# Batch 2's k and v as six tokens to a partition, with no fifth-slot load, and k's permutation in four pieces

## The chip, the cores and the metric

The kernel runs on one core of a Trainium2 chip. The metric is the device time of one execution in microseconds (us). Before the change the median of seven runs is 293.79 us, the lowest 292.74 us and the highest 295.01 us.

## What is computed

The inputs q, k, v have 8 batches, 8 heads, 576 tokens and 64 features to a head, in f32. The first stage is an attention without a softmax, the second a feed-forward block with a residual.

```python
kv  = einsum('bhsd,bhse->bhde', k, v)                # 64 x 64 for each batch and head
out = einsum('bhsd,bhde->bhse', q, kv)
out = out / sqrt(mean(out*out, -1) + 1e-6) * g_norm  # norm over the 64 features of a head
x   = out with the heads side by side                # 8 x 576 rows of 512
xn  = (x - mean) / sqrt(var + 1e-6) * g_ln           # layer norm over 512
y   = x + relu(xn @ w_ch1) @ w_ch2                   # 512 -> 2048 -> 512
```

## The kernel before

**Tiles.** The 4608 rows are 36 tiles of 128. A batch has 576 tokens: four full tiles (token slots 0 to 3 of a partition) and a half tile, the "fifth slot", of 64 tokens. Two neighbouring batches share one tile for their two half tiles, so tile 8 is the fifth slot of batches 0 and 1, and tiles 9 to 12 are batch 2's. The order of the tiles is batch 0's four (0 to 3), batch 1's four (4 to 7), tile 8, batch 2's four, batch 3's four, their shared tile, and so on. Tiles 0 to 7 go through the feed-forward one at a time ("fine" groups, L629), later ones in blocks of four (L644). The second product (`m2`, L663) is always by tile, in four groups of four matmuls.

**One batch.** GpSimd (POOL) loads q, k and v and casts them to bf16 on the way. k has to lie token slot first in `kp`. For batches 0 and 1 the load puts six consecutive tokens on each of 96 partitions (`kb`, `vb`), with all 576 tokens in one load, and a copy (`k_permute`, L404) brings k into `kp`. For batch 2 four tokens go on each of 128 partitions, 512 tokens in all, and the last 64 tokens come by a second small load, `load_fifth` (L262): k's straight into slot 4 of `kp`, v's into `v5`. The other 64 partitions of that slot of `kp` are zeroed by a memset on POOL (L760). From batch 3 on, `load_slots` (L275) writes k into `kp` slot by slot and no copy is needed. q of batch 2 comes into `qb` and is permuted by two copies on ScalarE (ACT) (`q_permute`, L410), and its half tile is loaded by a `load_fifth` too. `kv_mm` (L456) multiplies k by v: 6 matmuls with 96 rows to a pair of heads for batches 0 and 1 (24 in all), 5 with 128 rows for the others (20).

q is needed transposed, as `qT`. Batch 0's slots are turned on TensorE (PE). Batch 1's slots 2 and 3 are turned by one DMA transpose issued by SyncE (SP), and its slot 4 by another; `late_turns` holds that last one back, in the plan, behind a main group of the feed-forward (L999). Batch 2 is turned by one DMA transpose for all slots, after its permutes and q's fifth slot. `t_out` (L478) then multiplies `qT` by the batch's kv; tile 8 needs slot 4 of both batch 0 and batch 1, eight matmuls.

**What sets the order.** Nothing is ordered at run time: each engine has a fixed list, written out by `run_plan` (L108) before the kernel runs. A step has an engine, a planned occupation, a key (lower is more urgent) and the steps it depends on. At each turn the plan takes, on each engine, the step that can start first; among those that can start at the same moment the lowest key wins, and among equal keys the one that was added first. Loads and DMA transposes book a common planned server one after another, at rates written by hand (L193 and L314):

```python
rate6, rate4, rate1 = 400.0, 395.0, 305.0
begin = max(server, t + s.occ + lat)
server = begin + wk
s.done = begin + wk + tail
```

`lag` adds a number of microseconds to a load's planned arrival before ACT or PE may be planned to use it. A POOL load waits for the eighth load before it. The keys that matter below: the out matmuls of tile 8 and `kv_mm` of batch 2 both have key 40, which is also the key of the first `m2` group of tile 4, and ties go in the order in which the steps are added (that group, then tile 8's out, L838, then batch 2's `kv_mm`, L803). In the list each engine waits for the data of an instruction, with all that stands behind it.

Of the kernel before, what the change touches and what calls it, by code (L numbers as in the profile page):

```python
# [14 lines left out]
def kernel(  # L15
# [11 lines left out]
    nc = tc.nc  # L27
# [22 lines left out]
    NEAR = 0.35  # L50
    BANKS = {"mm": 4, "out": 2, "kvt": 2}
    WARM_FROM = 1.3
    HALVED = (0,)
    SCALED = (0, 1)
    SPLIT_STORE = (23, 25)
# [42 lines left out]
    def add(eng, occ, dur, key, deps, fn, dma=None, alloc=None, main=False, lag=0.0):  # L98
        s = Step()
        s.eng, s.occ, s.dur, s.key, s.fn = eng, occ, dur, key, fn  # L100
        s.deps = [d for d in deps if d is not None]
        s.dma, s.alloc, s.main, s.frees, s.behind = dma, alloc, main, None, None
        s.start = s.done = None
        s.lag = lag
        steps.append(s)
        return s
# [131 lines left out]
    kv_pack = [consts.tile([128, HP, 128], bf16, name=f"kv_pack{i}") for i in range(3)]  # L238

    def kv_view(buf, b):  # L240
        if b < 2:
            return buf[b % 2][0:96, :].rearrange("p (h t d) -> p h t d", h=H, t=6)
        return buf[b % 2][:, 0:H * 4 * D].rearrange("p (h t d) -> p h t d", h=H, t=4)

    def load_kv(buf, src, b, h0=0, h1=H):
        t = 6 if b < 2 else 4
        n = 576 if b < 2 else 512
        def fn():
            nc.gpsimd.dma_start(  # L249
                kv_view(buf, b)[:, h0:h1, :, :].rearrange("p h t d -> p h (t d)"),  # L250
                src[b, h0:h1, 0:n, :].rearrange("h (p t) d -> p h (t d)", t=t))
        return fn, n * (h1 - h0) * 256
# [9 lines left out]
    def load_fifth(dst, src, b):  # L262
        def fn():
            nc.gpsimd.dma_start(
                dst[fifth(b), :, :], src[b, :, 512:576, :].rearrange("h p d -> p h d"))
        return fn, 64 * H * 256
# [49 lines left out]
    load = {}  # L316
# [25 lines left out]
    def pool_load(name, fnb, rate=425.0, deps=()):  # L342
        fn, nb = fnb
        s = add_dma("POOL", 0, deps, fn, nb, rate)
        load.setdefault(name, []).append(s)
# [58 lines left out]
    def k_permute(eng, b, h0, h1):  # L404
        src = kv_view(kb, b)
        t = src.shape[2]
        copy(eng, kp[b % 2][0:src.shape[0], 0:t, h0:h1, :],
             src[:, h0:h1, :, :].rearrange("p h t d -> p t h d"))
# [46 lines left out]

    def kv_mm(b, hps):  # L456
        ps = psum.tile([128, HP, 128], f32, tag="kvt", name="kv_ps", bufs=BANKS["kvt"])
        p, last = (slice(0, 96), 5) if b < 2 else (slice(0, 128), 4)
        for hp in hps:
            for t in range(last + 1):  # L460
                nc.tensor.matmul(  # L461
                    ps[:, hp, :],
                    lhsT=kp[b % 2][p, t, 2 * hp:2 * hp + 2, :].rearrange("p h d -> p (h d)"),
                    rhs=(v5[b % 2][:, 2 * hp:2 * hp + 2, :] if b >= 2 and t == 4
                         else kv_view(vb, b)[:, 2 * hp:2 * hp + 2, t, :]),
                    start=(t == 0), stop=(t == last))
            att[b]["kv", hp] = ps
# [253 lines left out]
    def plan_batch(b):  # L721
        p = pos[FIRST[b]]
        ok = okey[FIRST[b]]
        kperm = []
        if b == 1:
            for h0, h1 in ((0, 4), (4, 8)):
                kperm.append(add("ACT", 1.2, 1.35, p - 18, load["k", 1],
                                 lambda h0=h0, h1=h1: k_permute(nc.scalar, 1, h0, h1)))
            for t in range(5):
                key = (p - 17 + 3 * t) if t < 4 else pos[8] - 40  # L730
                if t < 4:
                    qperm = add("ACT", *act_cost(512), key, load["q", 1],
                                lambda t=t: q_permute(nc.scalar, 1, t, t + 1))
                    qread = qperm
                else:
                    qperm = load["q", 1, 4][0]
                if t < 2:
                    add_q_turn_pe(1, t, [qperm, z1[1]], key + 1, ("DVE", "ACT")[t % 2])
                elif t > 2:
                    add_q_turn_dma(1, *((2, 4) if t == 3 else (4, 5)), [qperm, z1[1]],  # L740
                                   key + 1 if t == 3 else pos[8] - 29)
            vdeps = load["v", 1]
            adone[1]["qread"] = qread
            adone[1]["qfree"] = adone[1]["qT", 4][0]
        else:
            f = FIRST[b]
            def gate(n):

                if b >= 3:
                    m, i = divmod(n, 4)  # L750
                    pool_do(0.1, lambda: nc.gpsimd.tensor_copy(  # L751
                        mark, blk[m]["xT"][:, 0, i * 128:i * 128 + 1]), done[n]["xT"])
            def gate_turn():
                if b >= 3:
                    pool_do(0.1, lambda: nc.gpsimd.tensor_copy(
                        mark, att[b - 1]["qT"][:, 0, 0:1]), [adone[b - 1]["qfree"]])
            dk = [adone[b - 2]["kvmm"]]
            if b < 4:

                pool_do(0.5, lambda: nc.gpsimd.memset(kp[b % 2][no_fifth(b), 4, :, :], 0.0), dk)  # L760
            gate(f - 8 if b > 3 else 5)
            gate_turn()
            by_slot = b >= 3
            if by_slot:
                pool_load(("k", b), load_slots(kp[b % 2], k, b), rate1, dk)
            else:
                pool_load(("k", b), load_kv(kb, k, b), rate4, dk)
            pool_load(("k", b), load_fifth(kp[b % 2][:, 4, :, :], k, b), 180.0, dk)
            def some_q():
                gate(f - 7 if b > 3 else 6)  # L770
                if by_slot:
                    pool_load(("q", b), load_slots(qp[b % 2], q, b), rate1, [adone[b - 2]["qfree"]])
                else:
                    pool_load(("q", b), load_q(b, 0, 4), rate4, [adone[b - 1]["qread"]])
                pool_load(("q", b), load_fifth(qp[b % 2][:, 4, :, :], q, b), 180.0,
                          [adone[b - 2]["qfree"]])
            def some_v():
                gate(f - 6 if b > 3 else 7)
                pool_load(("v", b), load_kv(vb, v, b), rate4, dk)
                pool_load(("v", b), load_fifth(v5[b % 2], v, b), 100.0, dk)  # L780
            for load_some in (some_v, some_q) if b == 2 else (some_q, some_v):
                load_some()
            for h0, h1 in ((0, 4), (4, 8))[by_slot * 2:]:
                kperm.append(add("ACT", 0.85, 1.0, ok - 16, load["k", b][0:1] + dk,
                                 lambda h0=h0, h1=h1: k_permute(nc.scalar, b, h0, h1)))
            qperm = []
            for t0, t1 in ((0, 2), (2, 4))[by_slot * 2:]:
                qperm.append(add("ACT", 0.85, 1.0, ok - 14, load["q", b][0:1] + [
                    adone[b - 2]["qfree"]], lambda t0=t0, t1=t1: q_permute(nc.scalar, b, t0, t1)))
            for x in kperm + qperm:  # L790
                x.lag = 4.0 if b == 2 else 6.0
            kperm += load["k", b]
            turn = add_dma("SP", ok - 12, qperm + load["q", b] + (
                adone[b - 3].get("outs", []) if b >= 3 else []),
                           lambda: q_turn_dma(b), 2.6e3, 1.0, occ=2.98, lat=0.25, tail=0.42)
            for t in range(5):
                adone[b]["qT", t] = [turn]
            adone[b]["qfree"] = turn
            turn.lag = 5.0 if by_slot else 0.0
            adone[b]["qread"] = qperm[-1] if qperm else None  # L800
            vdeps = load["v", b]
        outs_before = adone[b - 3].get("outs", []) if b >= 3 else []
        s = add("PE", 1.12 if b > 1 else 1.34, 1.35 if b > 1 else 1.57, (p - 17.5 if b == 1 else ok - 4), vdeps + kperm,  # L803
                lambda: kv_mm(b, range(HP)), alloc="kvt")
        a = add("DVE", 0.34, 0.38, (p - 17 if b == 1 else ok - 2), [s, z1[4], z1[5]] + outs_before,
                lambda: kv_out(b, 0, HP, nc.vector, False))
        a2 = add("DVE", 0.34, 0.38, (p - 17 if b == 1 else ok - 2), [a], lambda: kv_out(b, 0, HP, nc.vector, True))
        s.frees = a2
        s.lag = 5.0 if b > 2 else 2.0 if b == 2 else 0.0
        adone[b]["kvmm"] = s  # L810
        adone[b]["kv"] = [a2]
# [243 lines left out]
```

## Time and profile before

| | |
|---|---|
| median of seven runs | 293.79 us |
| the profiled execution | 293.79 us, its span 292.0 us |
| granted TensorE clock | 1.00 |
| PE busy | 284.2 us of the span |
| VectorE (DVE), ScalarE (ACT), GpSimd (POOL) busy | 164.8, 142.5, 65.9 us |
| q and kb loads of 512 KB from issue to landing | 18.6 us and 17.9 us |
| 64 KB loads into `kp` (k's fifth slots), to landing | 7.9 us |

The profile's page has the busy time of each engine, the span in 40 slices, and the chain of work that ended last, followed back from the end. The trace gives each engine's instructions in order of time: start, length, engine, line, operation, tile written and read, count, and in brackets an idle time before it and what ended that. PE's lengths are modelled and overlap: back to back, a 128-column matmul starts some 0.056 us after the one before and a 512-column one some 0.216 us after. "PEld" is the load of the stationary operand, and SPq is SP's queue of DMA issues.

### The profile page before, as it was taken

What the parts mean: (1) busy time and instruction counts of PE and PEld (TensorE: products, weight loads), DVE (VectorE), ACT (ScalarE), POOL (GpSimd) and SP (SyncE); (2) the same over time, 40 slices, a digit from 0 to 9 for tenths busy, and PEclk for the clock granted to TensorE, in tenths of its full rate; (3) what the DMA queues carried; (4) which work ended last, traced back from release to release, by engine and by line L of the source; (5) the groups of instructions that cost most, each with busy time, mean ns of one, the idle gap of its engine ahead of it and who ended that gap; (6) DMA issues with size and microseconds to landing.
All of it is one profiled execution on the core that took longest, in us unless ns stands there. A gap on an engine that the chain in (4) does not pass through costs nothing.

```text
span 292.0 us, 5193 instructions
## 1 busy us (share of the span) xinstructions
PE 284.2 (97%) x2046; PEld 162.7 (56%) x2074; DVE 164.8 (56%) x362; ACT 142.5 (49%) x288; POOL 65.9 (23%) x93
## 2 busy tenths in 40 slices
PE   8999989999999999999999999999999999999995
PEld 6879844977745445444544445444544444444444
DVE  2596029487983997557655775477557755320022
ACT  2279955797756612761276127612761177017400
POOL 8974230107309004502260406000000000000000
PEclk9999999999999999999999999999999999999999
DMA  6999999958999978998999399912101310120012
GB/s 92 178 196 206 204 199 177 250 69 108 180 212 103 171 109 199 116 169 175 131 135 167 88 188 115 191 55 92 54 18 56 90 54 18 56 88 20 2 72 73
DMA packets 108716, 35.60 MB, mean 122 GB/s; under 512 B 87187, under 2 KB 104467, under 8 KB 108692
## 3 DMA queue, kind: packets, MB, share of 16 engines
q0 software_dynamic: 72624, 18.35, 66.0%
q1 hardware_dynamic: 35828, 16.79, 26.0%
q8 instruction: 16, 0.26, 0.4%
q10 hardware_dynamic: 240, 0.13, 0.2%
q14 instruction: 8, 0.07, 0.1%
HBM read 36.70 MB, written 9.44 MB: 158 GB/s over the span
## 4 chain that ended last, share of the span: by engine, by line
PE 85%; DMA 7%; POOL 6%; issue 1%; ACT 0%; DVE 0%; POOLq 0%
PE mm_ps L663 41%; PE mm_ps L644 33%; DMA qb<-in_q_dram 7%; PE mm_ps L629 5%; PE out_ps L484 3%; PE kv_ps L461 2%; POOL qp L270 1%; POOL w L354 1%; POOL vb L249 1%; POOL kb L249 1%; PE xT_ps L579 1%; POOL w L356 0%; PE qT_ps L420 0%; ACT qp L400 0%; POOL identity masks.py:197 0%
## 5 line engine op out<-in xcount | busy, mean ns | idle before, releaser
L663 PE MATMUL mm_ps<-w,m 128*128 128x512 bf16 (+2 forms) x592 | 128.1, 368 | 0.7
L644 PE MATMUL mm_ps<-xT,w 128*128 128x512 bf16 x436 | 100.0, 379 | 0.6
L651 ACT ACTIVATE m<-mm_ps 128x512 bf16<-128x512 f32 x112 | 66.8, 597 | 50.8 <-PE mm_ps L644 48.5
L663 PEld LDWEIGHTS <-m 128*128 128x128 bf16 x608 | 57.2, 98 | 60.6
L644 PEld LDWEIGHTS <-w 128*128 128x128 bf16 x448 | 43.1, 98 | 48.8
L519 DVE TENSOR_REDUCE ss<-sq 128x8 f32<-128x512 f32 (+1 forms) x37 | 24.8, 669 | 48.2 <-ACT sq L510 48.0
L670 DVE SCALAR_TENSOR_TENSOR x<-mm_ps,rstd,x 128x512 f32<-128x512 f32 (+2 forms) x38 | 27.2, 719 | 40.6 <-PE mm_ps L663 40.6
L510 ACT ACTIVATE sq<-out_ps 128x512 f32<-128x512 f32 (+1 forms) x37 | 21.6, 584 | 45.9 <-PE out_ps L484 45.9
L629 PE MATMUL mm_ps<-xT,w 128*128 128x128 bf16 x512 | 30.6, 219 | 0.0
L629 PEld LDWEIGHTS <-w 128*128 128x128 bf16 x512 | 29.2, 98 | 0.8
L572 DVE SCALAR_TENSOR_TENSOR xc<-x,mv,gl 128x512 bf16<-128x512 f32 (+1 forms) x38 | 27.3, 723 | 1.2
L514 DVE TENSOR_TENSOR xg<-out_ps,gn 128x512 f32<-128x512 f32 x34 | 23.2, 683 | 0.2
L636 ACT ACTIVATE m<-mm_ps 128x512 bf16<-128x512 f32 x32 | 18.4, 596 | 3.1 <-PE mm_ps L629 2.9
L751 POOL COPY mark<-xT 128x1 bf16<-128x1 bf16 x15 | 6.5, 431 | 57.0 <-DMA xT<-xc 51.5
L523 ACT ACTIVATE rms<-ss,eps_attn 128x8 f32<-128x8 f32 (+1 forms) x37 | 11.1, 300 | 14.4 <-DVE ss L519 14.3
L550 DVE TENSOR_TENSOR x<-xg,inv 128x512 f32<-128x512 f32 x24 | 16.6, 691 | 0.8
L566 DVE BATCH_NORM_STATS2 stats<-x 128x6 f32<-128x512 f32 x24 | 16.5, 690 | 0.5
L484 PEld LDWEIGHTS <-qT 128*128 128x128 bf16 x160 | 11.4, 98 | 6.5 <-ACT qT L400 0.5
L484 PE MATMUL out_ps<-kv_pack,qT 128*128 128x128 bf16 x160 | 14.5, 219 | 0.3
L472 DVE CAST kv_pack<-kv_ps 64x256 bf16<-64x256 f32 x14 | 5.9, 422 | 11.9 <-PE kv_ps L461 11.8
L461 PEld LDWEIGHTS <-kp 128*128 128x128 bf16 (+1 forms) x168 | 10.7, 102 | 2.4 <-issue 0.4
L461 PE MATMUL kv_ps<-vb,kp 128*128 128x128 bf16 (+1 forms) x144 | 11.3, 227 | 0.4 <-DMA vb<-in_v_dram 0.4
(69 smaller groups left out, 183.1 us busy)
## 6 DMA issues: line engine op xcount, KB each, us to landing
out_dram<-x SPq DMA_DIRECT2D x30, 256.0 KB, 2.6
w<-in_moe_w_ch_dram POOLq DMA_DIRECT2D x8, 512.0 KB, 12.2
vb<-in_v_dram POOLq DMA_DIRECT2D x6, 512.0 KB, 10.8
kp<-in_k_dram POOLq DMA_DIRECT2D x5, 512.0 KB, 8.5
qp<-in_q_dram POOLq DMA_DIRECT2D x5, 512.0 KB, 10.1
out_dram<-x SPq DMA_DIRECT2D x10, 128.0 KB, 2.3
qb<-in_q_dram POOLq DMA_DIRECT2D x2, 512.0 KB, 18.6
qp<-in_q_dram POOLq DMA_DIRECT2D x10, 64.0 KB, 9.0
```

Source lines behind the costliest of these rows:

```text
L461: nc.tensor.matmul(ps[:, hp, :], lhsT=kp[b % 2][p, t, 2 * hp:2 * hp + 2, :].rearrange("p h d -> p (h d)"), rhs=(v5[b % 2][:, 2 * hp:2 * hp ...
L484: nc.tensor.matmul(o3[:, hp, :], lhsT=att[b]["qT"][:, 4 * t + hp, :], rhs=kv_pack[b % 3][:, hp, :], start=(i == 0), stop=(i == len(bs) - 1))
L510: nc.scalar.activation(sq[:, h0:h1, :], st[n]["ps", h0][:, h0:h1, :], func=AF.Square)
L514: nc.vector.tensor_mul(xg[:, h0:h1, :], st[n]["ps", h0][:, h0:h1, :], gn.to_broadcast([128, h1 - h0, D]))
L519: nc.vector.tensor_reduce(ss[:, h0:h1, :], st[n]["sq"][:, h0:h1, :], axis=AX.X, op=ALU.add)
L572: nc.vector.scalar_tensor_tensor(xc[:, f0:f1], in0=st[n]["x"][:, f0:f1], scalar=blk[m]["mv"][:, i, 0:1], in1=gl[:, f0:f1], op0=ALU.subtrac ...
L629: nc.tensor.matmul(ps[:, d, :], lhsT=w1[c][:, kk, d * 128:(d + 1) * 128], rhs=blk[m]["xT"][:, kk, i * 128:(i + 1) * 128], start=(kk == 0), ...
L636: nc.scalar.activation(st[n]["m1"][:, c, :, :], st[n]["m1ps", c], func=AF.Relu)
L644: nc.tensor.matmul(ps, lhsT=w1[c][:, kk, d * 128:(d + 1) * 128], rhs=blk[m]["xT"][:, kk, :], start=(kk == 0), stop=(kk == nKm - 1))
L651: nc.scalar.activation(blk[m]["m1", c][:, d, :], blk[m]["m1ps", g], func=AF.Relu)
L663: nc.tensor.matmul(st[n]["m2ps", f0], lhsT=m1_piece(n, c, d), rhs=w2[c][:, d, f0:f1], start=(c == 0 and d == 0), stop=(c == 3 and d == 3))
L670: nc.vector.scalar_tensor_tensor(x[:, f0:f1], in0=st[n]["m2ps", f0], scalar=blk[m]["rstd"][:, i, :], in1=x[:, f0:f1], op0=ALU.mult, op1=AL ...
```

## The change

Batch 2 joins batches 0 and 1 in the form with six tokens to a partition. Its loads of k's and v's fifth slot are gone, `kv_mm` of batch 2 takes 24 matmuls of 96 rows, and `k_permute` is issued in four pieces of two heads in place of two of four. The memset of `kp`'s empty half slot, which was before batches 2 and 3, is before batches 3 and 4. In the plan the k load of batch 2 is booked at 400 (`rate6`), a k piece at 0.63 us with key ok - 13 in place of 0.85 us with ok - 16, and the lag of batch 2's k and q permutes is 3.0 in place of 4.0.

```diff
+    SIXES = 3
     def kv_view(buf, b):
-        if b < 2:
+        if b < SIXES:
             return buf[b % 2][0:96, :].rearrange("p (h t d) -> p h t d", h=H, t=6)
...
     def load_kv(buf, src, b, h0=0, h1=H):
-        t = 6 if b < 2 else 4
-        n = 576 if b < 2 else 512
+        t = 6 if b < SIXES else 4
+        n = 576 if b < SIXES else 512
...
     def kv_mm(b, hps):
-        p, last = (slice(0, 96), 5) if b < 2 else (slice(0, 128), 4)
+        p, last = (slice(0, 96), 5) if b < SIXES else (slice(0, 128), 4)
...
-                    rhs=(v5[b % 2][:, 2 * hp:2 * hp + 2, :] if b >= 2 and t == 4
+                    rhs=(v5[b % 2][:, 2 * hp:2 * hp + 2, :] if b >= SIXES and t == 4
...
-            if b < 4:
+            if b in (SIXES, SIXES + 1):
                 pool_do(0.5, lambda: nc.gpsimd.memset(kp[b % 2][no_fifth(b), 4, :, :], 0.0), dk)
...
-                pool_load(("k", b), load_kv(kb, k, b), rate4, dk)
-            pool_load(("k", b), load_fifth(kp[b % 2][:, 4, :, :], k, b), 180.0, dk)
+                pool_load(("k", b), load_kv(kb, k, b), rate6, dk)
+            if b >= SIXES:
+                pool_load(("k", b), load_fifth(kp[b % 2][:, 4, :, :], k, b), 180.0, dk)
...
                 pool_load(("v", b), load_kv(vb, v, b), rate4, dk)
-                pool_load(("v", b), load_fifth(v5[b % 2], v, b), 100.0, dk)
+                if b >= SIXES:
+                    pool_load(("v", b), load_fifth(v5[b % 2], v, b), 100.0, dk)
...
-            for h0, h1 in ((0, 4), (4, 8))[by_slot * 2:]:
-                kperm.append(add("ACT", 0.85, 1.0, ok - 16, load["k", b][0:1] + dk,
-                                 lambda h0=h0, h1=h1: k_permute(nc.scalar, b, h0, h1)))
+            for h0 in () if by_slot else (0, 2, 4, 6):
+                kperm.append(add("ACT", 0.63, 0.75, ok - 13, load["k", b][0:1] + dk,
+                                 lambda h0=h0: k_permute(nc.scalar, b, h0, h0 + 2)))
...
-                x.lag = 4.0 if b == 2 else 6.0
+                x.lag = 3.0 if b == 2 else 6.0
...
-        s = add("PE", 1.12 if b > 1 else 1.34, 1.35 if b > 1 else 1.57, ...
+        s = add("PE", 1.12 if b >= SIXES else 1.34, 1.35 if b >= SIXES else 1.57, ...
```

More of the change, by code (lines that the diff above doesn't have):

```diff
@@ L802, in plan_batch @@
         outs_before = adone[b - 3].get("outs", []) if b >= 3 else []
-        s = add("PE", 1.12 if b > 1 else 1.34, 1.35 if b > 1 else 1.57, (p - 17.5 if b == 1 else ok - 4), vdeps + kperm,
+        s = add("PE", 1.12 if b >= SIXES else 1.34, 1.35 if b >= SIXES else 1.57, (p - 17.5 if b == 1 else ok - 4), vdeps + kperm,
                 lambda: kv_mm(b, range(HP)), alloc="kvt")
```

## The prediction

> **What bounds the kernel now.** I read the page's busy times and its chain of work first.
>
> ```profile
> PE 284.2 (97%) x2046; PEld 162.7 (56%) x2074; DVE 164.8 (56%) x362; ACT 142.5 (49%) x288; POOL 65.9 (23%) x93
> PE 85%; DMA 7%; POOL 6%; issue 1%; ACT 0%; DVE 0%; POOLq 0%
> ```
>
> PE carries 85% of the chain. The DMA and POOL part is the start, and the chain in order of time shows where it ends:
>
> ```profile
> 19.51 19.90 DMA qb<-in_q_dram
> 39.43 0.63 ACT qp L400
> 40.06 0.05 issue
> 40.11 0.40 PE qT_ps L420 x4
> ```
>
> So PE's last wait for anything is for batch 1's q; PE's own order of time gives it as 0.71 us idle, from 39.4 us. From 40.11 to 288.6 us the chain never leaves PE but for gaps of 0.05 us. Every matmul added after 40 us is paid in full, every new PE wait too, and removing work elsewhere after 40 us earns nothing. What matters is which PE instruction has least time to spare around batch 2's loads. PE's order of time, the loads of PE's stationary operand, and SP's queue show it:
>
> ```profile
> 58.77 1.03 PE L663 MATMUL mm_ps<-w,m 128*128 128x512 bf16 x3
> 59.63 0.39 PE L461 MATMUL kv_ps<-vb,kp 128*128 128x128 bf16 x4
> ...
> 60.75 0.61 PE L484 MATMUL out_ps<-kv_pack,qT 128*128 128x128 bf16 x8
> ```
>
> ```profile
> 59.42 1.32 PEld L461 LDWEIGHTS <-kp 128*128 128x128 bf16 x20
> 60.70 0.49 PEld L484 LDWEIGHTS <-qT 128*128 128x128 bf16 x8
> ```
>
> ```profile
> 48.90 3.73 SPq L676 DMA_DIRECT2D out_dram<-x  x4
> 52.74 1.22 SPq L442 DMA_TRANSPOSE qT<-qp  x1
> ```
>
> ```profile
> qT<-qp SPq DMA_TRANSPOSE x1, 8.0
> ```
>
> The eight out matmuls at 60.75 us are tile 8's. They read `qT` of batch 1's slot 4, which that transpose writes: issued at 52.74, landing 8.0 us later, at about 60.7 us. PE's first `qT` load starts at 60.70. The transpose lands just in time, and only because `kv_mm` of batch 2 (20 matmuls, 1.12 us) runs ahead of it.
>
> **What the skill says.** "DMA: Bandwidth & Descriptors", section "Queues, rings and completion order": POOL's loads and SP's stores and transposes are different rings on the same 16 DMA engines, which take turns between rings by packets, each ring in its own order. The trace agrees: batch 2's q load (issued at 42.47 us, landing 17.4 us later) and this transpose, behind four stores, both finish near 60 us. The same page, "Specifications", says packets under 512 B are inefficient; the trace puts a modest number on it below. "ScalarE: Activation LUTs", "What ACT_TABLE_LOAD costs": 186 ns + 0.833 ns an element, with 93 ns overlapped back to back; k's copy of 1536 elements takes 1468 ns here, 1466 by that rule. "TensorE: Matmul & The Clock Gate", "Wait — 56ns, not 53.3ns?": 56 ns between warm 128-column matmuls; 1.12 us / 20 is the same.
>
> **The change part by part.**
>
> *Four more matmuls in `kv_mm`.* 24 x 0.056 = 1.34 us for 1.12: +0.22 us, on PE's path. The 96-row form in batch 1 takes the same spacing (24 matmuls from 34.44 to 35.78).
>
> *k's copies.* A piece of 768 elements: 186 + 640 - 93 = 0.73 us estimated from the skill's rule, four 2.93 us, against 1.98 us for two now: +0.95 us on ACT. They start at 49.44 us now, right behind ACT's work and 0.5 us after k's landing at 48.9. The next copy, tile 5's xT, starts at 52.27 after 0.85 us idle and PE wants it at about 55.2 us, so the cost is nothing. Without that cover, delay over 2.3 us would reach PE.
>
> *POOL.* Two 0.69 us issues and a 0.52 us memset leave the time before 52 us; POOL idles in that stretch for landings anyway. v's load takes the issue slot at 34.66 us for 36.99; q's stays behind batch 1's q copies at 42.47. Ring order makes the earlier issue worthless: landings are k1 30.7, v1 34.4, a weight 36.7, q1 39.4, k2 48.9 us (issue plus the time to landing, batch number behind the tensor). So the 0.71 us wait at 39.4 us is untouched. The memset returns before batch 4, where POOL then waits 7.55 us at a gate: nothing.
>
> *DMA work.* The bytes of k and v are the same: 64 KB more in each big load, two 64 KB loads gone. Only packet size gains. Two views of moving data, one with batch 0's and 1's q fifth slots in it and one without:
>
> ```profile
> DMA packets 1396, 0.42 MB, mean 182 GB/s; under 512 B 970, under 2 KB 1396, under 8 KB 1396
> ```
>
> ```profile
> DMA packets 605, 0.47 MB, mean 205 GB/s; under 512 B 13, under 2 KB 605, under 8 KB 605
> ```
>
> The first is 42.0 to 44.3 us, the second 37.0 to 39.3. At 205 GB/s its 0.42 MB would take 2.05 us, not 2.3, so two fifth slots cost some 0.25 us above their bytes. Bounds: below nothing (v1 took 3.7 us against k1's 3.0 and q1's 2.7, so a six-token load may cost 0.7 more than a four-token one in place of 0.33) and up to 2.4 us gained (k2's and v2's fifths landed 1.7 and 1.4 us after the load before, less 2 x 0.33). I take 0.27 us, because those two spacings include the stores.
>
> *The order.* Here lies the main cost. The plan, used for order alone, books k2 + fifth + v2 + fifth as 2.65 + 0.73 + 2.65 + 1.31 = 7.35 us, and now 2.95 + 2.99 = 5.94, so all that it books behind them, q, the stores and the slot-4 transpose, comes 1.41 us earlier in the plan, against 0.27 us in fact. In the plan of before, tile 8's out became ready while `kv_mm` of batch 2 (key 40, 1.12 us) ran: not earlier, since with an equal key and an earlier place in the list it would have gone first, and not later, since the next `m2` group (key 41) would have gone first. 1.41 us earlier is ahead of `kv_mm`'s start in every case. So tile 8's out goes before `kv_mm`, right behind tile 4's first `m2` group. PE will want `qT` at 60.70 - 1.12 = 59.58 us and have it at 60.70 - 0.27 = 60.43: a wait of 0.85 us. Behind it in PE's list is everything, and PE has no slack later to win it back.
>
> *q's copies.* Lag and bookings together plan them 2.41 us earlier, at some 58 us for 60.55, ahead of two ACT evictions, while q lands at about 59.6 (59.9 now). ACT waits some 1.6 us there. Evictions then come 2 to 3.5 us later; they were at 58.08 and 58.97 and their banks are wanted from about 65 us. Tile 6's xT is copied at 62.43 now and wanted at 64.01, which moves later with PE's own wait. I count nothing; it starts to cost if q lands after about 60.
>
> *Tile 9's out.* The plan moves it 2.35 us forward from 69.53. Batch 2's transpose would land near 66.5 for 67.5 now, PE reaches it after 67.4: nothing, with 0.9 us to spare.
>
> **Sum.** Profiled execution 293.79 us (span 292.0, and 1.79 around it) + 0.22 + 0.85 = 294.86 us. Its own time is the median of the runs, so 294.9 us stands for both, +0.36%. With the wait between 0.5 and 1.1 us the likeliest case spans 294.5 to 295.1.
>
> **Rivals.**
>
> *A, the transpose really comes earlier.* If the small packets cost what the fifths' landings suggest, the transpose lands 1.1 us or more sooner, by 59.58, and only the matmuls remain: 294.0 us, no measurable change. For it: 1.7 and 1.4 us between landings. Against it: 0.25 us for two fifths with no store beside them. It decides at 0.44 us of gain: there the wait is 0.66 us and the sum 0.88 us, 0.3%, which is about what a measurement of this kernel can tell. A plan that keeps `kv_mm` ahead gives the same time, since tile 8's out then comes 0.22 us later than now.
>
> *B, PE waits longer.* Tile 8's out goes one main group (0.86 us) further forward, or the six-token loads are slow and q's copies hold ACT until tile 6's xT is late. Place: PE between 57.9 and 65 us; price 0.9 us more: 295.75 us. For it: the 3.7 us of v1. Against it: the keys, which put tile 4's first group ahead.
>
> *C, faster.* The 0.71 us wait at 39.4 us goes: 293.79 - 0.71 + 0.22 = 293.3 us at best, and less than that only by luck between runs. Nothing in ring order speaks for it.
>
> **How the numbers follow.** Likeliest case 0.62, A 0.19, B 0.12, C 0.07. Of the likeliest, 0.52 lies beyond 0.3% and 0.10 within. Slower: 0.52 + 0.12 = 0.64; same: 0.10 + 0.19 = 0.29; faster 0.07. The range reaches from just under A, 293.9, to just over B, 296.0, and leaves C and a tail out.
>
> **What would show it.** Tile 8's eight out matmuls ahead of the 24 of `kv_ps`, with an idle stretch of PE near 59.6 us that ends on DMA `qT`; the transpose landing at 60.2 to 60.7 us; k's copies in four pieces of 0.83 us each, overlapping; q's copies first in ACT's list near 58 us after a wait for `qb`; PE dense after 61 us. It is wrong if PE stays dense through 58 to 62 us, or if the wait stands at another tile.

## The result, and the profile after

The changed kernel takes 295.35 us (median of 15 runs, 295.06 to 298.25) where the kernel before took 293.57 us (36 runs, 292.74 to 295.14): the ratio is 1.0065, 95% interval 1.0048 to 1.0081. It is slower, by some 1.8 to 1.9 us. The forecast was 294.9 us. The direction and the range hold, but the wait that was forecast is not the one that came: by the sign that the prediction itself gave (a wait at another tile), its mechanism is wrong.

The page of the changed kernel, busy times and the chain of work that ended last. In the lines shown, line numbers are one higher than before:

```profile
PE 284.0 (97%) x2050; PEld 162.1 (55%) x2078; DVE 165.1 (56%) x362; ACT 143.5 (49%) x290; POOL 66.0 (22%) x91
PE 74%; DMA 20%; DVE 2%; ACT 2%; issue 1%; POOL 0%; POOLq 0%
```

PE is as busy as before (the four matmuls are in its counts), the span grew from 292.0 to 293.9 us, and PE's share of the chain fell from 85% to 74%. Followed back from the end, the chain now leaves PE at 67.69 us and goes on through a transpose and ACT to batch 2's q load. PE's own order of time in the changed kernel (start, length, engine, line, what; in brackets an idle time and what ended it):

```profile
54.57 1.50 PE L462 MATMUL kv_ps<-vb,kp 96*128 96x128 bf16 x24
55.91 0.61 PE L485 MATMUL out_ps<-kv_pack,qT 128*128 128x128 bf16 x8
56.36 3.74 PE L630 MATMUL mm_ps<-xT,w 128*128 128x128 bf16 x64
61.13 1.02 PE L664 MATMUL mm_ps<-w,m 128*128 128x512 bf16 x3 [1.04 <-ACT m L637]
61.99 0.61 PE L485 MATMUL out_ps<-kv_pack,qT 128*128 128x128 bf16 x8
...
65.26 1.95 PE L630 MATMUL mm_ps<-xT,w 128*128 128x128 bf16 x32
67.69 0.40 PE L485 MATMUL out_ps<-kv_pack,qT 128*128 128x128 bf16 x4 [0.48 <-DMA qT<-qp]
```

Three things are to be seen. The 24 kv matmuls of batch 2 now stand at 54.57 us, ahead of tiles 6 and 7; before, they were at 59.63. PE then stops at tile 4's first `m2` group until an ACT eviction is done. And it stops again at tile 9's out for `qT`. Tile 8's out (61.99) waits for nothing. The 64 matmuls from 56.36 are through 64 x 0.0558 = 3.57 us later, at 59.93, so the first stop costs 61.13 - 59.93 = 1.20 us; the 32 from 65.26 are through at 67.05, so the second costs 0.64 us.

ACT's order of time in the changed kernel says why the eviction (L637) is late:

```profile
56.83 0.28 ACT L615 ACTIVATE std<-mv,eps_ln 128x1 f32<-128x1 f32 x1
58.60 1.99 ACT L401 COPY qp<-qb 128x1024 bf16<-128x1024 bf16 x2 [1.49 <-DMA qb<-in_q_dram]
60.49 0.59 ACT L637 ACTIVATE m<-mm_ps 128x512 bf16<-128x512 f32 x1
```

q's two copies stand ahead of the eviction of tile 5's first group in ACT's list. They wait 1.49 us for q, run 2.0 us, and only then is the eviction done, at 61.1 us. In the kernel before, all four of tile 5's evictions stood ahead of them (the last is shown), and they did not wait:

```profile
58.97 0.60 ACT L636 ACTIVATE m<-mm_ps 128x512 bf16<-128x512 f32 x1 [0.30 <-PE mm_ps L629]
...
60.55 1.99 ACT L400 COPY qp<-qb 128x1024 bf16<-128x1024 bf16 x2
```

There are four accumulators of this kind, taken in turn: tile 4 used all four, tile 5 takes them again, and tile 4's first `m2` group needs the one that tile 5's first group holds. PE's list had come to that group at 59.93.

The chain in order of time shows the second stop: batch 2's transpose is issued at 61.06 and takes 6.58 us.

```profile
58.60 1.99 ACT qp L401 x2
60.59 0.47 ACT m L637
61.06 6.58 DMA qT<-qp
67.64 0.05 issue
67.69 0.40 PE out_ps L485 x4
```

The chain puts an eviction just before the transpose. SP's own waits name another releaser, q's fifth slot, which landed at 60.94 us; q's copies had ended at 60.59:

```profile
SPq L443 <- DMA qp<-in_q_dram: 7.1, 1, 7.1
```

The account of the two profiled executions: PE starts tile 4's first feed-forward group 0.18 us earlier than before (50.77 for 50.95; nothing there was changed), then +0.22 for the matmuls, +1.20 and +0.64: 1.88 us, against 1.9 us between the spans.

One stretch of PE shows the loss without the start of the kernel: from the first matmul of tile 4's first feed-forward group (L629, in the changed kernel L630) to the first matmul of the first block of four tiles (L644, there L645). It takes 32.58 us before (50.95 to 83.53) and 34.66 us after (50.77 to 85.43), 2.08 us more. From its end to PE's last matmul it is 204.80 us in all eleven profiled executions of this document. What comes ahead of it took 50.05, 50.95 and 51.18 us in three executions that have the same lists up to there, so a good part of the difference between executions arises at the start.

### The profile page after: what moved, and what is told of

Read it like the earlier page. It is cut to its first block, busy times and chain, and to the rows that moved or that the text cites. A ratio compares the mean times of both kernels' runs of the same rounds, so it can differ in the third digit from the quotient of the medians.

```text
span 293.9 us, 5200 instructions
## 1 busy us (share of the span) xinstructions
PE 284.0 (97%) x2050; PEld 162.1 (55%) x2078; DVE 165.1 (56%) x362; ACT 143.5 (49%) x290; POOL 66.0 (22%) x91
## 4 chain that ended last, share of the span: by engine, by line
PE 74%; DMA 20%; DVE 2%; ACT 2%; issue 1%; POOL 0%; POOLq 0%
PE mm_ps L664 35%; PE mm_ps L645 32%; DMA qb<-in_q_dram 12%; DMA w<-in_moe_w_ch_dram 3%; PE out_ps L485 3%; DMA kb<-in_k_dram 2%; DMA qT<-qp 2%; PE kv_ps L462 2%; PE mm_ps L630 2%; ACT qp L401 1%; DVE x L671 1%; PE xT_ps L580 0%; POOL kb L250 0%; DVE stats L567 0%; DVE x L551 0%
## 5 line engine op out<-in xcount | busy, mean ns | idle before, releaser
L645 PE MATMUL mm_ps<-xT,w 128*128 128x512 bf16 x436 | 100.0, 379 | 0.6
L645 PEld LDWEIGHTS <-w 128*128 128x128 bf16 x448 | 43.1, 98 | 48.6
L630 PE MATMUL mm_ps<-xT,w 128*128 128x128 bf16 x512 | 30.6, 219 | 0.2 <-DMA w<-in_moe_w_ch_dram 0.2
L630 PEld LDWEIGHTS <-w 128*128 128x128 bf16 x512 | 29.2, 98 | 1.1 <-DMA w<-in_moe_w_ch_dram 0.4
L752 POOL COPY mark<-xT 128x1 bf16<-128x1 bf16 x15 | 8.8, 586 | 58.3 <-DMA xT<-xc 53.8
L637 ACT ACTIVATE m<-mm_ps 128x512 bf16<-128x512 f32 x32 | 18.3, 597 | 2.6 <-PE mm_ps L630 2.3
L524 ACT ACTIVATE rms<-ss,eps_attn 128x8 f32<-128x8 f32 (+1 forms) x37 | 11.1, 301 | 10.8 <-DVE ss L520 10.7
L250 POOL DMA_DIRECT2D vb<-in_v_dram x10 | 11.5, 1157 | 3.0 <-DMA vb<-in_v_dram 2.6
```

The lines of the kernel that those rows point to most:

```text
L630: nc.tensor.matmul(ps[:, d, :], lhsT=w1[c][:, kk, d * 128:(d + 1) * 128], rhs=blk[m]["xT"][:, kk, i * 128:(i + 1) * 128], start=(kk == 0), ...
L637: nc.scalar.activation(st[n]["m1"][:, c, :, :], st[n]["m1ps", c], func=AF.Relu)
L645: nc.tensor.matmul(ps, lhsT=w1[c][:, kk, d * 128:(d + 1) * 128], rhs=blk[m]["xT"][:, kk, :], start=(kk == 0), stop=(kk == nKm - 1))
```

## The experiments

The theory: the loss is PE's two stops and 0.22 us of matmuls, and the stops come from where the lists put q's copies and tile 9's out. The rival: the loads of six tokens and the matmuls over them cost it. Each ratio is to the kernel before on the same chip; "the stretch" is the one defined above, in the one profiled execution of each run.

**Tile 9's out further back.** In the plan, one line behind the out step:

```diff
+            o.lag = 1.5 if n == 9 else 0.0
```

> The changed kernel with one plan entry added: tile 9's out is planned 1.5 us after its transpose, which moves these four matmuls two main groups further back in PE's list and nothing ahead of them. Theory (two waits on PE, 1.2 us for an eviction at tile 4's first m2 group and 0.64 us for qT at tile 9, plus 0.22 us of matmuls): the second wait goes, the first stays at 1.2 us; 295.35 - 0.64 = 294.7 us, ratio to before 1.004. Rival (the loss lies in the loads and the matmuls themselves): no change, 295.35 us, ratio 1.0065.

Measured: 294.92 us, ratio 1.0050 (1.0030 to 1.0071). The direction fits, the size can't be told from the interval. The profiled execution, the fastest of the twelve (294.48 us), does not show what was expected: the eviction stop is missing too, and the stretch takes 32.80 us, 0.22 more than before. The order is that of the changed kernel, with q's copies ahead of all of tile 5's evictions, but here q landed at 56.06 us, before ACT came to the copies:

```profile
57.66 1.98 ACT L401 COPY qp<-qb 128x1024 bf16<-128x1024 bf16 x2
...
60.58 1.03 PE L664 MATMUL mm_ps<-w,m 128*128 128x512 bf16 x3
```

So the order alone doesn't stop PE; q must also land later than ACT comes to its copies. The run was repeated with the changed kernel beside it and the out one more group back (2.5 for 1.5):

> The changed kernel itself, on the same chip as the next run, so that the two can be set beside each other. 295.2 us, ratio 1.006.

> The changed kernel with tile 9's out planned 2.5 us after its transpose (1.5 in the first such run), so that it stands another main group further back on PE. Theory (0.64 us of the loss is tile 9's wait for qT): 0.4 to 0.65 us less than the changed kernel beside it, ratio to before 1.004, with the eviction wait at tile 4 still there. Rival (tile 9's wait only hides a later one): the same time as the changed kernel.

Measured: the changed kernel 295.33 us, ratio 1.0055 (1.0035 to 1.0075); tile 9 later still 294.85 us, ratio 1.0048 (1.0031 to 1.0066). 0.48 us between the two, as the theory has it, though the intervals overlap. In this second execution of the changed kernel the stops are shorter (0.76 and 0.36 us idle, against 1.04 and 0.48) and the stretch takes 34.25 us; the 1.20 and 0.64 us above are those of one execution. With tile 9 later still it takes 33.82 us. PE's order of time in that last run:

```profile
60.35 1.02 PE L664 MATMUL mm_ps<-w,m 128*128 128x512 bf16 x4 [0.86 <-ACT m L637]
...
68.91 0.61 PE L485 MATMUL out_ps<-kv_pack,qT 128*128 128x128 bf16 x8
```

The eviction stop is still there, the stop at tile 9 (now with tile 10, eight matmuls) is gone, and no later one took its place.

**q's copies further back.**

```diff
-                x.lag = 3.0 if b == 2 else 6.0
+                x.lag = (3.0 if x in kperm else 4.5) if b == 2 else 6.0
```

> The changed kernel with the planned lag of batch 2's q copies alone at 4.5 in place of 3.0 (k's stays 3.0). In the lists this puts q's two copies behind the eviction of tile 5's first group on ACT, and tile 9's out where the run with tile 9 later has it; kv_mm stays where the change put it. Theory: both waits on PE go, 0.22 us of matmuls and at most 0.2 us at tile 9 remain; 293.8 to 294.0 us, ratio 1.001. Rival (loads and matmuls): 295.35 us, ratio 1.0065. If the eviction wait has another cause than q's copies: as the run with tile 9 later, 1.004.

Measured: 293.80 us, ratio 1.0014 (1.0001 to 1.0027). PE and ACT in order of time:

```profile
54.60 1.50 PE L462 MATMUL kv_ps<-vb,kp 96*128 96x128 bf16 x24
...
56.39 3.74 PE L630 MATMUL mm_ps<-xT,w 128*128 128x128 bf16 x64
59.97 1.03 PE L664 MATMUL mm_ps<-w,m 128*128 128x512 bf16 x3
...
67.66 0.39 PE L485 MATMUL out_ps<-kv_pack,qT 128*128 128x128 bf16 x4
```

```profile
57.66 0.58 ACT L637 ACTIVATE m<-mm_ps 128x512 bf16<-128x512 f32 x1
...
58.46 1.99 ACT L401 COPY qp<-qb 128x1024 bf16<-128x1024 bf16 x2
```

The edit moves two things: one eviction stands ahead of q's copies, and tile 9's out stands two main groups further back, as in the first run. PE goes through 59.97 and through tile 9's out without a stop. Loads, layout, kv matmuls and k's four pieces are those of the changed kernel. About four fifths of the loss is gone (1.0065 to 1.0014, on different chips), and what is left can't be told from the 0.22 us (0.07%) of the matmuls; the stretch takes 32.80 us, 0.22 more than before. The rival falls. How the four fifths divide between the two moves, this run doesn't say; tile 9's out alone gave 0.48 us.

**The shorter lag alone.** The kernel before with `x.lag = 3.0 if b == 2 else 6.0`.

> The kernel before with the lag of batch 2's k and q copies at 3.0 in place of 4.0 and nothing else. Theory (it takes the lag and the earlier bookings together to put q's copies ahead of tile 5's first eviction): they stay behind all four evictions of tile 5, ACT waits some 0.5 us for q, tile 9's out comes about 1 us earlier and still after its qT; 293.6 us, ratio 1.000. Rival (the shorter lag alone does it): an eviction wait of about 1 us, ratio 1.003 or more.

Measured: 293.44 us, ratio 0.9995 (0.9978 to 1.0012). The lag alone does nothing: q's copies stay behind tile 5's evictions, and the stretch takes 32.58 us as before. It needs the planned bookings of the loads as well.

**k's copy in two pieces.**

```diff
-            for h0 in () if by_slot else (0, 2, 4, 6):
-                kperm.append(add("ACT", 0.63, 0.75, ok - 13, ...
-                                 lambda h0=h0: k_permute(nc.scalar, b, h0, h0 + 2)))
+            for h0 in () if by_slot else (0, 4):
+                kperm.append(add("ACT", 1.26, 1.4, ok - 13, ...
+                                 lambda h0=h0: k_permute(nc.scalar, b, h0, h0 + 4)))
```

> The changed kernel with k's copy in two pieces of four heads (planned at 1.26 us each, so the plan behind them is the same). Theory: the pieces cost PE nothing, the two waits stay; 295.2 to 295.4 us, ratio 1.006 to 1.0065. Rival (four pieces delay ACT enough to make the waits): at least half of the loss goes, ratio 1.003 or less.

Measured: 295.04 us, ratio 1.0048 (1.0032 to 1.0064). Both stops are there (0.77 us idle for the eviction, 0.71 for `qT`), and the stretch takes 34.62 us. The ratio is lower than expected, but the interval meets that of the changed kernel and excludes the rival's 1.003. The pieces are not the cause.

**The kv matmuls back behind tile 8's out.** The run with q's copies later, and in addition:

```diff
-        s.lag = 5.0 if b > 2 else 2.0 if b == 2 else 0.0
+        s.lag = 5.0 if b > 2 else 5.0 if b == 2 else 0.0
```

> The run with q's copies later (lag 4.5), and the planned lag of batch 2's kv matmuls at 5.0 in place of 2.0, which puts them back behind tile 8's out: PE's list is then tile 4's first m2 group, tile 8's out, the 24 kv matmuls, the order that the prediction had named. Three of tile 5's evictions come before q's copies. The prediction's step (tile 8's out wants qT at about 59.6 us, the transpose lands at about 60.5): a PE wait of 0.85 us on DMA qT besides the 0.22 us of matmuls; 294.6 us, ratio 1.0035. Rival (the transpose is in time there too): 293.8 us, ratio 1.001, as with q's copies later alone.

Measured: 294.54 us, ratio 1.0034 (1.0018 to 1.0050). PE in order of time, and the transpose of batch 1's slot 4, issued at 51.59 us:

```profile
57.62 1.03 PE L664 MATMUL mm_ps<-w,m 128*128 128x512 bf16 x4
58.48 0.22 PE L485 MATMUL out_ps<-kv_pack,qT 128*128 128x128 bf16 x1
59.11 0.56 PE L485 MATMUL out_ps<-kv_pack,qT 128*128 128x128 bf16 x7 [0.41 <-DMA qT<-qp]
59.51 1.50 PE L462 MATMUL kv_ps<-vb,kp 96*128 96x128 bf16 x24
```

```profile
qT<-qp SPq DMA_TRANSPOSE x1, 7.5
```

The first of tile 8's matmuls reads batch 0's `qT`; the second reads batch 1's and waits until 59.11, when the transpose has just landed (51.59 + 7.5). 59.11 - 58.54 = 0.57 us is lost in this execution, and the stretch takes 33.38 us, 0.58 more than with q's copies later alone. So the forecast wait is real where the list has that order. Its price of 0.85 us isn't settled: the ratios of the two runs differ by 0.0020, some 0.6 us, on different chips and with intervals that overlap. The changed kernel doesn't have that order.

**The cause put into the kernel before.** Four-token loads and 20 matmuls, q's copies alone planned early:

```diff
-                x.lag = 4.0 if b == 2 else 6.0
+                x.lag = (4.0 if x in kperm else 0.5) if b == 2 else 6.0
```

> The kernel before, four-token loads and 20 matmuls, with the planned lag of batch 2's q copies alone at 0.5 in place of 4.0. That puts them ahead of all four evictions of tile 5 on ACT, and the kv matmuls ahead of tile 4's first m2 group on PE. Theory (it is q's copies ahead of an eviction, not the layout): ACT waits for q from about 57 to 59.8 us, the first eviction ends at about 62.3 us, PE is through its kv matmuls at 59.9 and waits 2.4 us for a bank; 296 us, ratio 1.008. Rival (the six-token layout is needed for the loss): 293.5 us, ratio 1.000.

Measured: 296.28 us, ratio 1.0090 (1.0055 to 1.0125). ACT and PE in order of time:

```profile
59.21 1.99 ACT L400 COPY qp<-qb 128x1024 bf16<-128x1024 bf16 x2 [3.63 <-DMA qb<-in_q_dram]
```

```profile
61.75 1.02 PE L663 MATMUL mm_ps<-w,m 128*128 128x512 bf16 x4 [2.60 <-ACT m L636]
```

The same stop at the same instruction, 2.60 us long because q's copies stand further ahead of q (ACT waits 3.63 us for it). The stretch takes 35.46 us. No six-token load is needed for it.

**Can the old wait at 39.4 us be had?** The kernel before, batch 1's q in two loads around a weight's:

```diff
+        pool_load(("q", 1), load_q(1, 0, 2), rate4, [])
         load_w(1, 2)
-        pool_load(("q", 1), load_q(1, 0, 4), rate4, [])
+        pool_load(("q", 1), load_q(1, 2, 4), rate4, [])
...
-                    qperm = add("ACT", *act_cost(512), key, load["q", 1],
+                    qperm = add("ACT", *act_cost(512), key, load["q", 1][t // 2:t // 2 + 1],
                                 lambda t=t: q_permute(nc.scalar, 1, t, t + 1))
+                    qperm.lag = 0.8 if t < 2 else 0.0
```

> The kernel before with batch 1's q in two loads of two token slots, the first ahead of the second m2 weight's load and the second behind it; the plan after 42 us is the one of before. If the 0.7 us wait of PE at 39.4 us can be had by order alone: the first half lands near 36 us, the weight near 38.2, PE is dense from 35 to 42 us; 292.9 us, ratio 0.998. Rival (the stream of loads is full and the wait moves to the weight or to the smaller packets): 293.5 us, ratio 1.000.

Measured: 293.82 us, ratio 1.0021 (1.0002 to 1.0040): not faster, rather slower. In the profiled execution the wait is gone (PE goes from 34.23 to 67 us with no idle that is named), but that execution, 293.17 us, is the fastest of the fourteen, and a missing wait says little: in two others with the kernel before's lists up to there, the run with the shorter lag and the one with q's copies first, it is absent in the one and 0.41 us in the other. What the other thirteen lose isn't known. No version tried beats the kernel before.

## Why the prediction was right or wrong

*What bounds the kernel.* Right. PE's list is dense after 40 us and every new wait was paid in full: the two stops and the matmuls, 2.06 us, are the 2.08 us by which the stretch grew.

*Four more matmuls, +0.22 us.* Right: 24 in 1.34 us (54.57 to 55.91).

*k's copies, nothing.* Right. 3.03 us for the four, 2.93 estimated from the Trainium skill, "ScalarE: Activation LUTs", "What ACT_TABLE_LOAD costs", and tile 5's xT is copied at 52.22 for 52.27 before. The run with two pieces agrees.

*POOL, nothing.* Right, but q's issue came at 41.72 us, not 42.47.

*DMA work, 0.27 us for the transpose.* Wrong for both loads that it was applied to. The slot-4 transpose gained nothing (issued at 52.55, landing 8.2 us later, at 60.75 us), and q gained 1.3 us (58.6 for 59.9) in this pair of executions. q's fifth slot, right behind q in POOL's ring, gained nothing either (60.94 for 60.73), and batch 2's transpose needs it.

*The order.* This step failed. It held that the kv matmuls stay where their key puts them and that tile 8's out goes ahead of them. With both plans written out: the slot 2 and 3 transpose of batch 1 is planned to land at 53.81 us, not 1.41 us earlier than before but 1.25 later (52.56), because q's load is now asked for at the same planned moment and booked first. So at 53.82 neither tile 6's and 7's outs nor tile 5's first group (its accumulator is still held) can start in the plan, and the kv matmuls can: their v is planned without the fifth load, at 50.59 for 52.00, and its lag of 2.0 is over. They fill the hole. A key decides among steps that can start together; which steps these are, the prediction took over from the old plan. Tile 8's out does stand right behind tile 4's first `m2` group, as forecast, but 1.34 us of matmuls had moved ahead of both, and the wait of 0.85 us vanished. The run with the kv matmuls back behind shows it where the order is as forecast.

*q's copies, counted as nothing.* This is the term that was missed. The step had ACT's wait right (1.6 forecast, 1.49 in the trace, though it came about 1 us earlier) and the accumulators wrong: two evictions behind the copies, with banks "wanted from about 65 us". The list has four behind them, for two reasons that the written-out plans show: tile 5's groups were moved back 1.34 us by the kv matmuls, and q's copies come 3.43 us earlier (56.33 for 59.76), not 2.41, because q's load is now booked ahead of the slot 2 and 3 transpose. The first eviction's accumulator is wanted at 59.93. It is rival B's place (ACT held by q's copies, between 57.9 and 65 us), with an eviction in place of tile 6's xT and with q early, not late; its price there, 0.9 us, was 1.20.

*Tile 9's out, 0.9 us to spare.* Wrong by 1.5 us. PE came to it at 67.05, not after 67.4, and the transpose landed at 67.64, not near 66.5: it was issued at 61.06 and took 6.6 us, where before it was issued at 62.57 and landed by 67.5. (In the plan its out moves 3.5 us forward, not 2.35.) No edit tried why it took longer, but the DMA records of the changed kernel from 61.06 to 67.64 us show part of it (queue, packets, MB, share of the 16 engines' time):

```profile
q1 hardware_dynamic: 2592, 0.66, 53.9%
q8 instruction: 1, 0.02, 0.9%
```

The transpose's 256-byte packets start up to 4.55 us after its issue, in the kernel before up to 4.38. In the changed kernel one 16 KB packet of the queue that the profile calls "instruction" then takes 0.93 us, and the last two of the 4-byte writes that follow the data come behind it, at 5.5 us. The same packet, 0.88 to 0.96 us long, stands at this place in all six profiled executions whose lists have q's copies ahead of all of tile 5's evictions, and there the transpose took about 6.6 us. In the five others the packet comes within 1 us of the issue or not at all, and the transpose took at most 5.0 to 5.7 us. That the packet delays the transpose is argued from this, not shown by an edit; about half a microsecond more, and why the packet falls there, stay open.

*The sum.* 0.22 + 0.85 = 1.07 us forecast, 0.22 + 1.20 + 0.64 = 2.06 us found. The forecast of "slower" came out for a reason that was only partly its own: plans that run ahead of the data, at one place named wrongly and at two counted as nothing. That 294.9 us lies so near 295.35 is in good part luck: a wait that didn't come stood in for two that did.

## What to carry to other kernels

Where each engine's order is fixed ahead, an edit to loads works mostly through the order that a planner makes of the new arrival times; write both orders out and compare them before pricing anything. Then look in each list for an instruction that waits for a load and ask whose buffers are freed behind it: copies that came 1.5 us before their data cost PE 1.2 us through an eviction, and moving them behind one eviction, with tile 9's out two groups back, took back about four fifths of the loss. A planned lag belongs to one load in one order; changed together with the bookings it must be measured again. And where executions differ at the start, compare one stretch of the bounding engine: here it gave the 0.22 us of four matmuls, which the medians could not.

## What the runs showed of the hardware

Two small loads were taken out of POOL's ring, with the same bytes in the big ones. The next load of that ring, q, then landed sooner behind k: 9.5 us after it in the median of seven profiled executions (7.9 to 10.4), against 10.7 us in four with the small loads (9.7 to 11.0). The gain was hardly passed on. q's fifth slot, the load behind q, took 9.9 us from its issue against 10.2 (medians), and SP's slot-4 transpose 8.1 against 8.0.

A DMA transpose of five slots took at most 5.0 us from its issue in two executions and about 6.6 us in six, with no load of POOL's issued beside it; in the six, one 16 KB packet of the instruction queue, some 0.9 us long, stood ahead of its last two 4-byte writes.
